# Six PSUM banks handed out first-free-first, in place of a rotating pool

## The chip, the cores and the metric

One Trainium2 chip, one of its cores. A core has a matrix engine (TensorE, PE in the profile, with the loading of its stationary operand as PEld), VectorE (DVE), ScalarE (ACT), GpSimd (POOL) and a queue that issues most of the loads (SyncE, SP). They run their own lists of instructions in order and wait for each other through semaphores. The results of PE go to PSUM, which has eight banks of 128 x 512 words; DVE and ACT read them from there. The metric is the device time of one launch in microseconds; the time before is the median of three runs, 481.18 us (481.16 to 481.39).

## What is computed

An RWKV-6 attention over 4 batches, 8 heads, 768 steps and a head size of 48, and behind it an MLP mixer over tokens and channels:

```python
for t in range(S):                       # S = 768
    cur = einsum('bhd,bhe->bhde', u[None] * k_t, v_t)
    y[:, :, t] = einsum('bhd,bhde->bhe', r_t, state + cur)
    state = w_t[:, :, :, None] * state + einsum('bhd,bhe->bhde', k_t, v_t)
x = y.transpose(0, 2, 1, 3).reshape(4, 768, 384)
h = maximum(x.transpose(0, 2, 1) @ w_tok1, 0.0) @ w_tok2     # 768 -> 256 -> 768
u = x + h.transpose(0, 2, 1)
out = u + maximum(u @ w_ch1, 0.0) @ w_ch2                    # 384 -> 1536 -> 384
```

## The kernel before

The attention is cut into twelve units (`unit(i)`), three to a batch, each of 256 steps in four chunks of 64. In a unit PE turns the keys (`turned_keys`, L344, two banks `k_ps`), adds keys times values to a running state (`outer`, L364, in a bank of its own, `kv_ps`), multiplies keys with queries (`grams`, L314, two banks `gram`), and forms the output from the states (`across`, L379) and from inside the chunk (`within`, L400), both in two banks `y_ps`. ACT copies the turned keys out (L349) and the output into the tile x (L406); DVE masks the grams (L487) and runs the scans over the decay (L434, L442) and the long multiplications (L439, L445).

The mixer of batch 0 is `mixing`. Those of batches 1 to 3 are `exact_mixing`, which splits float32 factors into rounded parts (names with `forms`, `high`, `low`, `joint`), so that each product is three cheaper passes. In its channel part each of twelve column blocks takes one bank `ends_ps` with nine matmuls: L739 and L741 (`end_passes`), L746 (`joint_passes`). ACT reads that bank with a rectification (L721, `high_of`), then DVE reads it once more (L728, `low_of`), and with that the bank is free. `down` (L757 to L759) sums six blocks into one bank `o_ps`, which DVE adds to x (L765). `back_half` (L693) fills banks `h_ps`, read by DVE (L696); `turn` (L708) fills banks `xT_ps`, read by ACT (L710) and DVE (L711). The third factor of L741 and L758 comes from memory through a ring of ten places (`load_third`, L625), a load being issued when PE has used up an earlier one.

The three units of batch 0 aside (batches are counted from 0), all of this runs interleaved: `first_mixing`, `exact_mixing`, `attention_pieces` and others give streams of pieces. A piece is a key, a function that issues instructions, and a list of operations (engine, time, what it needs, and behind that the names of the banks it takes; `("free", name)` where a bank is done with). The string `ORDER` says which stream gives the next piece; `interleaved` puts them in that order, and `strict` makes every engine keep it. Before the change `interleaved` uses only the function of each piece and drops the operations with their bank names.

The part ahead of L1061 (attention of batch 0 and the first mixer steps) uses two pools of two. At L1061 these are closed, and from there on one pool `ps_m` with six rotating buffers serves every allocation: `bank(name)` and some direct `ps_m.tile(...)` calls. The n-th allocation takes the bank of the (n-6)-th, and its first matmul waits until that one's last reader is done, whether other banks are free or not.

## Time and profile before

| | us |
|---|---|
| median of three runs | 481.18 |
| the profiled execution | 481.39 |
| its span, first to last instruction | 479.7 |
| PE busy | 460.9 |
| DVE busy | 337.8 |
| ACT busy | 255.6 |
| PE waiting for the first load of rk | 8.3 |
| PE waiting after 52 us (one wait) | 1.5 |

The span is shorter than the time by what lies around the first and last instruction. A row of the timeline gives start and duration in us, engine, line and operation, what is written from what, how many instructions are merged, and in brackets how long the engine was idle and what ended it. A row of the waits names who waited for whom, the total, how often, and the longest.

### The profile page before, as it was taken

To read this page: it belongs to the slowest core of one execution; us is meant where nothing else is said; L and a number is where in the kernel's file an instruction comes from. 1 tells how busy PE (TensorE), PEld (TensorE's weight loads), DVE (VectorE), ACT (ScalarE), POOL (GpSimd) and SP (SyncE) were. 2 spreads that over 40 slices of the span, in tenths; PEclk is the share of its full clock that TensorE was granted. 3 is DMA by queue.
4 is the path that set the end of the run, shared out by engine and by line. 5 is a ranking of instruction groups with operands and counts; after the bars stand their busy time and mean duration, and the time that the engine had idled before them with its cause. 6 is when DMAs were issued, how large, how long until landed. Compare 5 with 4: busy or idle time off the path is not lost.

```text
span 479.7 us, 12681 instructions
## 1 busy us (share of the span) xinstructions
PE 460.9 (96%) x5298; PEld 405.1 (84%) x5298; DVE 337.8 (70%) x478; ACT 255.6 (53%) x588; POOL 59.8 (12%) x58
## 2 busy tenths in 40 slices
PE   3799999999999999999998999999999999999995
PEld 2686588856797668999998979999999979999995
DVE  7999799898786687675596966677596556235341
ACT  6689776765777566351546555251747344134140
POOL 1000000000000001240404001250404003032130
PEclk9889999999999999999999999999999999999999
DMA  8855653855563747854577723394585412336331
GB/s 310 327 198 193 215 194 105 264 188 185 175 182 105 241 131 227 232 179 150 183 239 235 268 75 117 123 267 134 163 276 169 166 37 82 118 98 198 88 94 55
DMA packets 49407, 83.77 MB, mean 175 GB/s; under 512 B 4864, under 2 KB 40576, under 8 KB 49344
## 3 DMA queue, kind: packets, MB, share of 16 engines
q1 hardware_dynamic: 49056, 82.80, 54.2%
q8 instruction: 43, 0.70, 0.6%
q14 instruction: 20, 0.16, 0.1%
q10 hardware_dynamic: 288, 0.10, 0.1%
HBM read 71.87 MB, written 11.01 MB: 173 GB/s over the span
## 4 chain that ended last, share of the span: by engine, by line
PE 93%; ACT 3%; DMA 1%; issue 1%; SPq 0%; DVE 0%; DVEq 0%; ACTq 0%
PE h_ps L953 10%; PE o_ps L757 8%; PE ends_ps L746 8%; PE ends_ps L739 8%; PE ends_ps L741 8%; PE o_ps L759 8%; PE o_ps L758 8%; PE z_ps L942 7%; PE h_ps L662 5%; PE gram L314 4%; PE z_ps L938 3%; PE h_ps L693 3%; PE y_ps L400 2%; PE kv_ps L364 2%; PE y_ps L379 2%; PE k_ps L344 2%
## 5 line engine op out<-in xcount | busy, mean ns | idle before, releaser
L732 POOL TENSOR_TENSOR z_high<-z_high 128x384 fp32r<-128x384 f32 x48 | 58.6, 1227 | 403.9 <-DMA ring<-third 187.7
L721 ACT ACTIVATE z_high<-ends_ps 128x384 fp32r<-128x384 f32 x48 | 23.5, 490 | 62.9 <-PE ends_ps L746 62.6
L728 DVE SCALAR_TENSOR_TENSOR z_high<-ends_ps,z_high 128x384 fp32r<-128x384 f32 x48 | 26.4, 554 | 36.7 <-ACT z_high L721 36.7
L739 PE MATMUL ends_ps<-x_forms,forms 128*128 128x384 f32 x216 | 50.0, 339 | 1.5 <-DVE z_high L728 1.5
L500 ACT ACTIVATE before<-state,to_end 112x48 f32<-112x48 f32 x132 | 33.3, 325 | 31.8 <-DVE state L515 20.0
L746 PE MATMUL ends_ps<-z_more,forms 128*128 128x384 f32 x216 | 50.1, 340 | 0.0
L741 PE MATMUL ends_ps<-x_forms,ring 128*128 128x384 f32 x216 | 49.3, 337 | 0.0
L953 PE MATMUL h_ps<-wch,z 128*128 128x384 f32 x144 | 48.5, 489 | 0.0
L757 PE MATMUL o_ps<-forms,z_high 128*128 128x384 f32 x140 | 48.2, 344 | 0.0
L765 DVE SCALAR_TENSOR_TENSOR x<-o_ps,x 128x384 f32<-128x384 f32 x35 | 18.7, 551 | 40.5 <-PE o_ps L759 40.4
L759 PE MATMUL o_ps<-forms,z_high 128*128 128x384 f32 x140 | 47.2, 337 | 0.0
L758 PE MATMUL o_ps<-ring,z_high 128*128 128x384 f32 x140 | 47.1, 337 | 0.0
L953 PEld LDWEIGHTS h_ps<-wch,z 128*128 128x128 f32 x144 | 26.7, 190 | 17.0
L739 PEld LDWEIGHTS ends_ps<-x_forms,forms 128*128 128x128 f32 x216 | 38.4, 188 | 2.2 <-DVE z_high L728 1.8
L746 PEld LDWEIGHTS ends_ps<-z_more,forms 128*128 128x128 f32 x216 | 39.0, 188 | 0.0
L741 PEld LDWEIGHTS ends_ps<-x_forms,ring 128*128 128x128 f32 x216 | 38.5, 188 | 0.0
L942 PE MATMUL z_ps<-xT,wch 128*128 128x256 f32 x144 | 31.5, 380 | 0.0
L942 PEld LDWEIGHTS z_ps<-xT,wch 128*128 128x128 f32 x144 | 27.1, 190 | 3.7
L724 ACT ACTIVATE z_high<-z_high 128x384 fp32r<-128x384 f32 x48 | 25.3, 526 | 3.5
L757 PEld LDWEIGHTS o_ps<-forms,z_high 128*128 128x128 f32 x140 | 26.3, 188 | 0.3
L758 PEld LDWEIGHTS o_ps<-ring,z_high 128*128 128x128 f32 x140 | 26.3, 188 | 0.0
L759 PEld LDWEIGHTS o_ps<-forms,z_high 128*128 128x128 f32 x140 | 26.3, 188 | 0.0
(198 smaller groups left out, 927.0 us busy)
## 6 DMA issues: line engine op xcount, KB each, us to landing
ring<-third SPq DMA_DIRECT2D x144, 192.0 KB, 3.1
raw<-in_w_ch_dram SPq DMA_DIRECT2D x16, 512.0 KB, 4.7
rk<-in_rk_dram SPq DMA_DIRECT2D x36, 192.0 KB, 5.4
near<-in_near_dram SPq DMA_DIRECT2D x8, 768.0 KB, 5.3
w<-in_w_dram SPq DMA_DIRECT2D x10, 520.5 KB, 4.1
vt<-in_v_dram SPq DMA_DIRECT2D x12, 384.0 KB, 4.6
out_dram<-x SPq DMA_DIRECT2D x17, 192.0 KB, 2.6
third<-forms SPq DMA_DIRECT2D x12, 192.0 KB, 3.1
```

What stands on the lines that cost most here:

```text
L500: act.mul(t[:ROWS, a], state[bt, g][:ROWS, a], by_last(c, j)[:, a:a + 1])
L724: act.mul(z_form(jt, 2), z_form(jt, 0).bitcast(f32), 1.0 / BASE)
L728: dve.scalar_tensor_tensor(z_form(jt, 1), a, 0.0, z_form(jt, 0).bitcast(f32), op0=ALU.max, op1=ALU.subtract)
L732: pool.tensor_add(z_form(jt, 2), z_form(jt, 2).bitcast(f32), z_form(jt, 1).bitcast(f32))
L739: pe.matmul(a, up[m], xf(0)[:, m], start=m == 0, stop=False)
L741: pe.matmul(a, low[:, m], xf(1)[:, m], start=False, stop=False)
L746: pe.matmul(banks["a", jt], joint, xf(2)[:, m], start=False, stop=m == 2)
L757: pe.matmul(a, z[0], up, start=first, stop=False, skip_group_check=True)
L758: pe.matmul(a, z[1], held[bt, s, half, 1, jt], start=False, stop=False, skip_group_check=True)
L759: pe.matmul(a, z[2], joint, start=False, stop=last, skip_group_check=True)
L942: pe.matmul(ps, now["wch1"][:, m, ts(jt, 128)], xT[:, m, ts(s, SEG)], start=(m == 0), stop=(m == DM // 128 - 1))
L953: pe.matmul(ps, zs[s][:, jt, ts(n, 128)], now["wch2"][:, jt, :], start=(jt == 0), stop=(jt == NJ - 1))
```

## The change

After L1061 the pool has one buffer of each name, and six tiles, `bank0` to `bank5`, are made from it once and put in a list. `with_banks` wraps the function of each piece: it sets the names of the banks that the piece takes, `bank` pops the first of the list for each, and after the piece the banks named in its `free` operations go to the end of the list. The direct `ps_m.tile` calls of `mixing` go through `bank` as well. Waits now follow from the accesses to the six tiles, not from the release of a pool's buffer. Lines behind the new functions stand 22 or more further down (L739 is now L761, L746 is L768, L344 is L366).

```diff
+    free_banks, taken_as, due = [], {}, []
+
     def bank(name):
-        return ps_m.tile([128, 512], f32, name=name, tag="m")
+        if not free_banks:
+            return ps_m.tile([128, 512], f32, name=name, tag="m")
+        t = free_banks.pop(0)
+        if due:
+            taken_as.setdefault(due.pop(0), []).append(t)
+        else:
+            free_banks.append(t)
+        return t
+
+    def with_banks(key, f, ops):
+        names = [(key[0], n) for op in ops if op[0] != "free" for n in op[3:]]
+
+        def g():
+            due[:] = names
+            f()
+            assert not due
+            for op in ops:
+                if op[0] == "free":
+                    free_banks.append(taken_as[key[0], op[1]].pop(0))
+
+        return g
...
-                sums[i] = ps_m.tile([128, DM], f32, name="h1_ps", tag="m")
+                sums[i] = bank("h1_ps")[:, :DM]
...
-                ps = ps_m.tile([128, DM], f32, name="h_ps", tag="m")
+                ps = bank("h_ps")[:, :DM]
...
-                sums["z", s] = ps_m.tile([128, SEG], f32, name="z_ps", tag="m")
+                sums["z", s] = bank("z_ps")[:, :SEG]
...
-                sums[n] = ps_m.tile([128, DM], f32, name="h2_ps", tag="m")
+                sums[n] = bank("h2_ps")[:, :DM]
...
-        out = [next(left_of[int(n)])[1] for n in order]
+        out = [with_banks(*next(left_of[int(n)])) for n in order]
...
-    ps_g, ps_m = None, six_banks.enter_context(tc.tile_pool(name="ps_m", bufs=6, space=bass.MemoryType.PSUM))
+    ps_g, ps_m = None, six_banks.enter_context(tc.tile_pool(name="ps_m", bufs=1, space=bass.MemoryType.PSUM))
+    free_banks += [ps_m.tile([128, 512], f32, name=f"bank{n}") for n in range(6)]
```

No engine's instructions change their number or order (PE's 3471 matmuls among them). What changes is the bank that a group gets and the semaphores that its first instruction waits for. Two places on PE show it; the numbers behind the names are the tiles'.

The first is in the last of the four parts of six blocks that the channel mixer of batch 1 has: two key tiles are turned, and two blocks follow, the third and fourth of the part. Before:

```order
L344 MATMUL k_ps_3029<-ident_101,rk1_89 128x112 [waits DMAHW7_49,DMAHW0_49,DVE_49]
L344 MATMUL k_ps_3029<-ident_101,rk1_89 128x112 x3
L344 MATMUL k_ps_3030<-ident_101,rk1_89 128x112 x4
L739 MATMUL ends_ps_3052<-x_forms_1343,forms1_1298 128x384 [waits DVE_49]
L739 MATMUL ends_ps_3052<-x_forms_1343,forms1_1298 128x384 x2
L741 MATMUL ends_ps_3052<-x_forms_1343,ring2_2230 128x384 [waits DMAHW4_49]
L741 MATMUL ends_ps_3052<-x_forms_1343,ring2_2230 128x384 x2
L746 MATMUL ends_ps_3052<-z_more_2116,forms1_1298 128x384 x3
L739 MATMUL ends_ps_3067<-x_forms_1343,forms1_1298 128x384 [waits DVE_49]
```

And with the change:

```order
L366 MATMUL bank5_886<-ident_101,rk1_89 128x112 [waits DMAHW7_49,DMAHW0_49,DVE_49]
L366 MATMUL bank5_886<-ident_101,rk1_89 128x112 x3
L366 MATMUL bank4_885<-ident_101,rk1_89 128x112 [waits Activation_49]
L366 MATMUL bank4_885<-ident_101,rk1_89 128x112 x3
L761 MATMUL bank1_882<-x_forms_1307,forms1_1263 128x384 [waits DVE_49]
L761 MATMUL bank1_882<-x_forms_1307,forms1_1263 128x384 x2
L763 MATMUL bank1_882<-x_forms_1307,ring2_2148 128x384 [waits DMAHW4_49]
L763 MATMUL bank1_882<-x_forms_1307,ring2_2148 128x384 x2
L768 MATMUL bank1_882<-z_more_2042,forms1_1263 128x384 x3
L761 MATMUL bank5_886<-x_forms_1307,forms1_1263 128x384 [waits Activation_49]
```

The last row is the same matmul in both: before it waited for DVE, now it writes the bank that the first turned keys had a few rows above, and waits for ACT.

The second place is the last block of the same part in batch 2. Before:

```order
L746 MATMUL ends_ps_4415<-z_more_2116,forms1_1298 128x384 x3
L739 MATMUL ends_ps_4429<-x_forms_1343,forms1_1298 128x384 [waits DVE_49]
L739 MATMUL ends_ps_4429<-x_forms_1343,forms1_1298 128x384 x2
L741 MATMUL ends_ps_4429<-x_forms_1343,ring2_2230 128x384 [waits DMAHW4_49]
L741 MATMUL ends_ps_4429<-x_forms_1343,ring2_2230 128x384 x2
```

And with the change:

```order
L768 MATMUL bank1_882<-z_more_2042,forms1_1263 128x384 x3
L761 MATMUL bank4_885<-x_forms_1307,forms1_1263 128x384 [waits Activation_49]
L761 MATMUL bank4_885<-x_forms_1307,forms1_1263 128x384 x2
L763 MATMUL bank4_885<-x_forms_1307,ring2_2148 128x384 [waits DMAHW4_49]
L763 MATMUL bank4_885<-x_forms_1307,ring2_2148 128x384 x2
```

Here too a wait for DVE became one for ACT: the bank was a `y_ps` before, and ACT copies that out.

## The prediction

> **What bounds the kernel now.** I read the page first, for the engine that is never free and for the chain that ended last.

> ```profile
> span 479.7 us, 12681 instructions
> ...
> PE 460.9 (96%) x5298; PEld 405.1 (84%) x5298; DVE 337.8 (70%) x478; ACT 255.6 (53%) x588; POOL 59.8 (12%) x58
> ...
> PE 93%; ACT 3%; DMA 1%; issue 1%; SPq 0%; DVE 0%; DVEq 0%; ACTq 0%
> ```

> TensorE (PE) is busy for 460.9 of 479.7 us and holds 93% of the chain. The change touches neither the number nor the size of any matmul, so it can give or take only idle time of PE. Next came the busy time by stage. The stretch up to 52 us is the part before the six banks are set up, which the change does not reach.

> ```profile
> core 0: us, PE busy (x) PEld busy (x) DVE busy (x) ACT busy (x) POOL busy (x), PEclk, DMA share, GB/s
> 0.00:52.00 52.00, 39.85 (x1004) 30.13 (x1005) 45.37 (x51) 39.70 (x100) 1.27 (x10) 0.93 0.75 263
> 52.00:187.00 135.00, 134.89 (x1457) 100.11 (x1457) 114.36 (x147) 91.29 (x191) 0.00 (x0) 1.00 0.57 176
> 187.00:254.00 67.00, 67.00 (x670) 66.28 (x669) 46.77 (x72) 31.66 (x83) 17.34 (x13) 1.00 0.66 205
> 254.00:257.00 3.00, 1.50 (x9) 1.18 (x8) 2.69 (x3) 2.04 (x7) 1.28 (x2) 1.00 0.68 160
> 257.00:479.70 222.70, 217.64 (x2165) 207.41 (x2163) 128.55 (x208) 90.95 (x211) 39.94 (x35) 1.00 0.46 144
> ...
> 474.30 0.34 PE L781 MATMUL o_ps<-ring,z_more 128*128 128x384 f32 x1
> ```

> From 52 us on PE has 0.11 us free, then none, then 1.50 us between 254 and 257 us, then 5.06 us. The last is the tail: the last matmul ends at 474.30 + 0.34 = 474.64, which is 5.06 us before the end of the span. The granted clock is 1.00 all through. So the stage that the change reaches has a single hole. The view of waits, restricted to PE after 52 us, has one row, and it is that hole:

> ```profile
> PE ends_ps L739 <- DVE z_high L728: 1.5, 1, 1.5
> ```

> **What the hole is.** L739 is the first matmul of a new group; it reads x_forms and forms, long there, and starts a new bank. So the wait on VectorE's L728 (which writes z_high, but reads the old ends_ps) is a wait for a bank. The timeline around it:

> ```profile
> 250.49 0.70 PE L746 MATMUL ends_ps<-z_more,forms 128*128 128x384 f32 x3
> 251.22 0.49 ACT L721 ACTIVATE z_high<-ends_ps 128x384 fp32r<-128x384 f32 x1 [0.47 <-PE ends_ps L746]
> 251.55 2.32 DVE L442 TENSOR_TENSOR_SCAN w<-w,starts 112x1041 f32<-112x1041 f32 x1
> 252.84 0.86 ACT L349 COPY kT<-k_ps 128x384 f32<-128x384 f32 x2
> 253.90 1.86 DVE L445 TENSOR_TENSOR rk<-rk,w 112x1024 f32<-112x1024 f32 x1
> 254.09 0.69 PE L746 MATMUL ends_ps<-z_more,forms 128*128 128x384 f32 x3
> 255.68 1.01 DVE L728 SCALAR_TENSOR_TENSOR z_high<-ends_ps,z_high 128x384 fp32r<-128x384 f32 x2
> 256.28 0.79 PE L739 MATMUL ends_ps<-x_forms,forms 128*128 128x384 f32 x3 [1.50 <-DVE z_high L728]
> 257.45 0.69 PE L746 MATMUL ends_ps<-z_more,forms 128*128 128x384 f32 x3
> 257.97 0.68 PE L739 MATMUL ends_ps<-x_forms,forms 128*128 128x384 f32 x3
> 259.53 0.68 PE L739 MATMUL ends_ps<-x_forms,forms 128*128 128x384 f32 x3
> ```

> The group that ended at 250.49 + 0.70 = 251.19 was read by ScalarE (ACT) at 251.22, but its second reader, L728 on VectorE, stood behind a 2.32 us scan and a 1.86 us multiplication and began only at 255.68. In round-robin order that bank's turn came at the group of 256.28, five allocations later (two y, two k, one ends), so PE stood until L728 had read it.

> **The change part by part.** Nothing moves: every engine has the same instructions in the same order, on VectorE and the load queue with the same waits. What changes is which bank an allocation gets, and so which reader it waits for: 72 PE instructions, 45 on ACT, two on POOL.

> *Term 1, the hole.* In the new list that group takes the bank of k_ps, which the first of the two L349 copies frees at about 252.84 + 0.43 = 253.27. PE could go on as soon as it is done with the group before: L746 started at 254.09, and three matmuls at the group's own rhythm (257.97 to 259.53 is nine in 1.56, 0.173 each) put the next start at 254.61. 256.28 - 254.61 = 1.67; the profile's idle, counted from the modelled end, is 1.50. I take 1.6 us. The bounds from both sides are 0, if the next wait is as long, and 1.67 + 0.11 = 1.78, all idle time of that stage.

> *Where the stall goes.* Does PE, 1.6 us earlier, run into the next late read? The group of 257.97 becomes 256.37 and takes the bank of the second L349 copy, free at 252.84 + 0.86 = 253.70: 2.67 us to spare. The group of 259.53 becomes 257.93 and takes the very bank that was late. It is free after the first L728 of the pair, at 255.68 + 0.55 = 256.23, so 1.7 us to spare, and 1.24 even against the end of the pair at 256.69. Behind them stand sets of matmuls that themselves drive their readers: the readers come 1.6 us earlier too, since ACT is busy for 90.95 and VectorE for 128.55 of the last 222.70 us. Loads cannot be the next limit at once: PE has no wait on a DMA in that row of waits, and the ring loads are issued by what PE has finished, so they move with it.

> *Term 2, the other changed waits of PE.* For each one I took the end of the reader it now names, in the trace of before, and the start of the matmul. None would have held PE. The two closest are these:

> ```profile
> 364.73 0.47 ACT L406 COPY x<-y_ps 64x384 f32<-64x384 f32 x1
> 366.18 0.69 PE L739 MATMUL ends_ps<-x_forms,forms 128*128 128x384 f32 x3
> ...
> 284.45 0.56 DVE L671 SCALAR_TENSOR_TENSOR z_more<-h_ps,z_more 128x384 fp32r<-128x384 f32 x1 [0.79 <-ACT z_more L669]
> 285.74 1.38 PE L693 MATMUL h_ps<-z_more,z_high 128*128 128x384 f32 x7
> ```

> At 366.18 the group now takes a y bank, which ACT's last copy frees at 364.73 + 0.47 = 365.20: 0.98 us to spare. At 286.09 (the third L693 of its row, two steps of 0.173 after 285.74) the bank is free at 284.45 + 0.56 = 285.01: 1.08 us to spare. Cost 0; the cover is that 1 us, and if it were gone, each place would cost what ACT or VectorE is late beyond it.

> *Term 3, ACT and POOL.* ACT gets 13 more entries in its lists of waits (mostly L710, which now also names VectorE's last read of the same bank). The closest is this pair:

> ```profile
> 287.33 1.61 DVE L696 SCALAR_TENSOR_TENSOR x<-h_ps,x 128x384 f32<-128x384 f32 x3 [1.73 <-PE h_ps L693]
> 290.41 0.49 ACT L710 ACTIVATE x_forms<-xT_ps 128x384 fp32r<-128x384 f32 x1 [0.36 <-PE xT_ps L708]
> ```

> L696 ends at 287.33 + 1.61 = 288.94, 1.47 us before L710 starts, and PE itself had to see the same read before it wrote the bank. Cost 0, covered by ACT's free 131.75 us of the last 222.70; if that cover were gone, each of the 13 could at most double the 0.36 us that such an L710 already stands there for, 4.7 us of ACT in all, still a small part of what it has free.

> *Sum.* The profiled execution took 481.39 us, with 1.69 us around its span; 481.39 - 1.6 = 479.79. The median of the three runs shown is 481.18, 0.21 below the profiled one; 481.18 - 1.6 = **479.6 us**. A measurement of this kernel can tell about 0.2% from no change, 0.96 us, so the line between faster and same lies at 480.22.

> **The rivals.** *A: the gain is mostly taken back at the next late read.* For it: VectorE is at its fullest there, 2.69 of 3.00 us, and PE has used up the lead that let it run ahead. Against it: the margins of 2.67, 1.7 and 1.24 us. If VectorE comes to that pair later by one more scan (2.32 us), the group of 259.53 waits 2.32 - 1.24 = 1.08 us, and of the 1.6 only 0.52 is left: 481.18 - 0.52 = 480.7 us. That counts as no change.

> *B: slower, because a bank comes back sooner than in strict rotation.* The mechanism: first-free-first goes by the order of the pieces, not by the time at which a reader is done, and can hand a y or k bank to an ends group soon after its copy is issued. Place: the attention units, where a y bank is passed to an ends group (366.18, margin 0.98; in round-robin the same group waited for an L728 that had ended at 363.12, 3.07 us before). It decides once ACT's copies come later than now by more than 0.98 us. Price: one hole such as today's, 1.50 us, at every second of the six units of the last two batches: 3 x 1.5 - 1.6 = 2.9, so 484.1 us; for one such hole the balance is 481.18 - 1.6 + 1.5 = 481.1. Against it: between 187 and 474 us ACT is busy for under half of the time, and its order has not changed.

> [...]

> *C: the change does nothing here*, because the wait at 256.28 has a second condition as late as L728. For it: a wait is put down to the last of several. Against it: in the order of before, the only wait on that L739 is for VectorE. 481.2 us.

> **How the numbers follow.** My forecast, 479.6 us, gets 0.79 and its own range is 479.2 to 480.2 (1.78 us and the 0.2 us by which the runs differ on one side, the line of 480.22 on the other). Rival A has 0.11, C has 0.03, B has 0.07, of which 0.02 for the single hole that leaves no change. Faster 0.79, same 0.11 + 0.03 + 0.02 = 0.16, slower 0.05. The range takes the forecast and most of A: 479.2 to 480.7 us.

> **What would show it.** Right: the view of PE's waits after 52 us is empty; the group of 256.28 starts near 254.6; every later matmul stands 1.6 us earlier; the busy time of PE is still 460.9; the tail is still 5.06. Wrong step by step: a new row of PE waiting on L728 or L406 (A or B), the row still there (C), or matmuls of the same line that take longer than now. The forecast as a whole falls if PE's busy time changes by more than half a microsecond, for then banks matter to the matmuls themselves, of which no row of before tells anything.

## The result and the profile after

The changed kernel took 479.34 us (median of 22 runs) beside 481.34 us for the one before in the same 22 rounds; the ratio, with disturbed runs left out, is 0.9952 with a 95% interval of 0.9936 to 0.9967. Two more sets of 12 runs of the same kernel gave 0.9973 (0.9957 to 0.9988) and 0.9968 (0.9953 to 0.9983). Weighted by their runs the three make 0.9962, or 1.8 us of 481.2. The forecast was 1.6 us faster, 479.6; by the first set alone 481.18 x 0.9952 = 478.9, which is under the low end of 479.2.

The page of the changed kernel, its chain by engine among it:

```profile
span 479.1 us, 12687 instructions
...
PE 459.6 (96%) x5298; PEld 404.6 (84%) x5298; DVE 338.0 (71%) x478; ACT 255.8 (53%) x588; POOL 59.8 (12%) x58
...
PE 92%; DMA 3%; ACT 2%; issue 1%; DVE 1%; SPq 1%; DVEq 0%; ACTq 0%
```

By stage (columns as in the table of the prediction; L761 is L739 of before, L768 is L746, L336 is L314):

```profile
0.00:52.00 52.00, 38.34 (x1002) 29.31 (x1003) 44.64 (x50) 38.99 (x100) 1.27 (x10) 0.97 0.77 264
52.00:187.00 135.00, 135.00 (x1458) 100.07 (x1457) 114.83 (x148) 91.85 (x190) 0.00 (x0) 1.00 0.56 176
187.00:254.00 67.00, 65.88 (x660) 65.02 (x659) 45.53 (x71) 30.30 (x77) 15.74 (x13) 1.00 0.66 200
254.00:257.00 3.00, 3.00 (x22) 3.00 (x22) 2.97 (x2) 3.00 (x12) 2.28 (x1) 1.00 0.98 257
257.00:479.10 222.10, 217.41 (x2164) 207.18 (x2162) 130.01 (x211) 91.62 (x213) 40.51 (x35) 1.00 0.47 145
```

The 1.50 us that PE lacked between 254 and 257 us are filled. But the stretch ahead of it, full before, now lacks 1.12. The view of PE's waits after 52 us has again one row, another one:

```profile
PE bank L336 <- issue: 1.1, 1, 1.1
```

"issue" is time in which the engine waited for nothing that the profile shows. The timeline has it in the middle of a row of grams, where no bank begins and no semaphore is waited for:

```profile
239.21 0.54 PE L336 MATMUL bank<-rk 48*64 48x64 f32 x21
240.87 0.85 PE L336 MATMUL bank<-rk 48*64 48x64 f32 x41 [1.12 <-issue]
```

And this is the place of the old hole, 1.6 us later in the span because of that pause and of the first 52 us:

```profile
253.15 2.32 DVE L464 TENSOR_TENSOR_SCAN w<-w,starts 112x1041 f32<-112x1041 f32 x1
254.44 0.86 ACT L371 COPY kT<-bank 128x384 f32<-128x384 f32 x2
255.50 1.86 DVE L467 TENSOR_TENSOR rk<-rk,w 112x1024 f32<-112x1024 f32 x1
255.70 0.69 PE L768 MATMUL bank<-z_more,forms 128*128 128x384 f32 x3
256.22 0.69 PE L761 MATMUL bank<-x_forms,forms 128*128 128x384 f32 x3
257.29 0.55 DVE L750 SCALAR_TENSOR_TENSOR z_high<-bank,z_high 128x384 fp32r<-128x384 f32 x1
```

VectorE comes to its late read (L750, L728 of before) behind the same scan and the same multiplication, only at 257.29; PE's next group began at 256.22, 0.52 us after the start of the last three matmuls ahead of it, and did not wait.

Laid over each other matmul by matmul (PE's order is the same in both), the two traces differ in few places. Start in the change less start before, in us, and the step at each place:

```
at before   line   difference   step
  45.71     L896      +0.69     +0.80   the first 52 us, pause "issue"
 151.62     L314      +0.26     -0.29   grams, pause "issue"
 239.27     L314      +1.60     +1.33   grams, pause "issue"
 256.28     L739      -0.06     -1.67   the hole
 256.56     L739      -0.17     -0.11   the matmuls behind the hole, 0.79 to 0.69
 span end             -0.59
```

So the hole was worth 1.67 + 0.11, unrounded 1.77 us. In this one execution a pause at a matmul that begins no bank, 1.33 us longer here than in the profile of before, took most of it back. The medians show that this execution, 480.81 us, was slower than most of its kernel.

### The profile page after: what moved, and what is told of

It is laid out like the page before. It is cut to its first block, busy times and chain, and to the rows that moved or that the text cites. A ratio compares the mean times of both kernels' runs of the same rounds, so it can differ in the third digit from the quotient of the medians.

```text
span 479.1 us, 12687 instructions
## 1 busy us (share of the span) xinstructions
PE 459.6 (96%) x5298; PEld 404.6 (84%) x5298; DVE 338.0 (71%) x478; ACT 255.8 (53%) x588; POOL 59.8 (12%) x58
## 4 chain that ended last, share of the span: by engine, by line
PE 92%; DMA 3%; ACT 2%; issue 1%; DVE 1%; SPq 1%; DVEq 0%; ACTq 0%
PE bank L975 10%; PE bank L768 8%; PE bank L761 8%; PE bank L779 8%; PE bank L763 8%; PE bank L781 8%; PE bank L780 8%; PE bank L964 7%; PE bank L684 5%; PE bank L960 3%; PE bank L715 3%; PE bank L336 2%; PE bank L401 2%; PE bank L422 2%; PE kv_ps L386 2%; DMA w<-in_w_dram 2%
## 5 line engine op out<-in xcount | busy, mean ns | idle before, releaser
L750 DVE SCALAR_TENSOR_TENSOR z_high<-bank,z_high 128x384 fp32r<-128x384 f32 x48 | 26.4, 553 | 35.0 <-ACT z_high L743 35.0
L768 PE MATMUL bank<-z_more,forms 128*128 128x384 f32 x216 | 50.1, 340 | 0.0
L761 PE MATMUL bank<-x_forms,forms 128*128 128x384 f32 x216 | 49.9, 339 | 0.0
L763 PE MATMUL bank<-x_forms,ring 128*128 128x384 f32 x216 | 49.4, 337 | 0.0
L975 PE MATMUL bank<-wch,z 128*128 128x384 f32 x144 | 48.5, 489 | 0.0
L779 PE MATMUL bank<-forms,z_high 128*128 128x384 f32 x140 | 48.2, 344 | 0.0
L781 PE MATMUL bank<-forms,z_high 128*128 128x384 f32 x140 | 47.2, 337 | 0.0
L780 PE MATMUL bank<-ring,z_high 128*128 128x384 f32 x140 | 47.1, 337 | 0.0
L975 PEld LDWEIGHTS bank<-wch,z 128*128 128x128 f32 x144 | 26.7, 190 | 17.0
L768 PEld LDWEIGHTS bank<-z_more,forms 128*128 128x128 f32 x216 | 39.0, 188 | 0.0
L761 PEld LDWEIGHTS bank<-x_forms,forms 128*128 128x128 f32 x216 | 38.5, 188 | 0.4
L763 PEld LDWEIGHTS bank<-x_forms,ring 128*128 128x128 f32 x216 | 38.6, 188 | 0.0
L746 ACT ACTIVATE z_high<-z_high 128x384 fp32r<-128x384 f32 x48 | 25.3, 526 | 3.8 <-ACT z_high L743 0.4
L779 PEld LDWEIGHTS bank<-forms,z_high 128*128 128x128 f32 x140 | 26.3, 188 | 0.3
L781 PEld LDWEIGHTS bank<-forms,z_high 128*128 128x128 f32 x140 | 26.3, 188 | 0.0
```

Of the source, the lines that this page charges most:

```text
L746: act.mul(z_form(jt, 2), z_form(jt, 0).bitcast(f32), 1.0 / BASE)
L750: dve.scalar_tensor_tensor(z_form(jt, 1), a, 0.0, z_form(jt, 0).bitcast(f32), op0=ALU.max, op1=ALU.subtract)
L761: pe.matmul(a, up[m], xf(0)[:, m], start=m == 0, stop=False)
L763: pe.matmul(a, low[:, m], xf(1)[:, m], start=False, stop=False)
L768: pe.matmul(banks["a", jt], joint, xf(2)[:, m], start=False, stop=m == 2)
L779: pe.matmul(a, z[0], up, start=first, stop=False, skip_group_check=True)
```

## What the words ahead of the prediction had wrong

They say that the pool of before hands the bank of the (n-6)-th allocation to the n-th. It does not. These are the first eleven allocations after L1061 as the built program of before has them:

```
tile  h  h  xT h  xT h  xT h  xT z  z
bank  2  7  6  5  4  3  2  6  4  7  5
```

In rotation the eighth would be bank 7. It is bank 6, of the first xT, which ACT has read by 56.00 us in the trace, while bank 7 is read by VectorE until 56.74; 4 (56.38) comes next, then 7, then 5 (57.20). And around the hole the two y banks, still in use, are passed over. Here the pool followed the order in which the banks in fact came free, which neither of the two rules of this document does. At the hole it did not: it gave out the bank that VectorE read at 255.68 ahead of the two that ACT had read by 253.70. The explanation of the hole from the trace does not depend on the rule; the word "round-robin" in the prediction is wrong. Over the 261 allocations after L1061 the bank is that of the sixth allocation before in 51% of the cases; with the change it is so in 48%.

## The experiments

**Both lists of banks, with and without the one late bank.** The first kernel has the six fixed tiles, but each allocation takes the bank that it had before, from a written list. In it and in the second, one bank passes on before its last read in the order of the pieces: at the first unit of batch 3 the copy of the turned keys (L349) reads what the next group has put there, so batch 3 is computed from other keys, with the same work. The copy starts at 286.40 us where before has 284.31; PE does not wait for it.

```diff
-        t = free_banks.pop(0)
...
-        return t
+        return free_banks[int(next(in_order, 0))]
...
-        out = [with_banks(*next(left_of[int(n)])) for n in order]
+        out = [next(left_of[int(n)])[1] for n in order]
```

> The six tiles are made once, but every allocation gets the bank that it had before the change, from a written list. Theory (the whole gain is the one hole at 256 us): the hole of 1.5 us on PE's L761 is back, ratio to before 1.000. Rival (the way the waits are derived, from accesses to six fixed tiles and not from the release of a pool's buffers, gives a part of its own): faster than before by about 0.5 us, ratio 0.999, with the hole still there.

Ratio 1.0008 (0.9990 to 1.0026). The hole is back, in PE's waits after 52 us:

```profile
PE bank L749 <- DVE z_high L738: 1.5, 1, 1.5
```

The second kernel exchanges two numbers of that list from the block at 256 us on, so that the order of the banks changes only there.

> The same list with one exchange: the block at 256 us takes the bank of the turned keys, the next block the bank that is read late; from there on the two numbers are exchanged. Theory: all of the gain, no wait of PE after 52 us, ratio 0.9965 (1.67 us of 481.2) or a little less. Rival (the gain is spread over many changed waits): 0.999 to 1.000, and the hole moves to the next block.

Ratio 0.9970 (0.9951 to 0.9988), and no wait of PE after 52 us at all. One bank exchanged for another in one place out of 261 brings what the whole change brings. The third starts from the list of the change and gives the late bank back to that block:

> The list of banks that the change gives, with one exchange: the block at 256 us takes the late bank again. Theory: the hole of 1.5 us is back and the time is that of before, ratio 1.000. Rival (72 changed waits each give a little): the gain stays but for the hole, ratio about 0.998.

Ratio 1.0005 (0.9990 to 1.0021), with the same wait of 1.5 us. So the other changed waits bring nothing that these intervals can tell, and neither do the fixed tiles.

**The changed kernel again**, twice, for the spread and the pause.

> The changed kernel once more, for a second profile and a second set of times. Theory: no wait of PE on a bank; the 1.1 us for which PE stood in the middle of the grams at 239.8 us in the first profile, with nothing to wait for, is not there again, and the ratio is 0.9963, above the 0.9952 of the first set. Rival (the first set was right as it stands): 0.995.

> The changed kernel a third time, for a third profile and a third set of times. Theory (hole of 1.77 us gone, pause amid the grams 0.4 to 1.3 us in this kernel and near 0 in the one before): ratio 0.996 to 0.9985 by the terms, no wait of PE on a bank after 52 us. Rival (the first set as it stands): 0.995.

The ratios stand at the top. In all three profiles the hole is gone by the same step of 1.67 us, and the pause is there in each, of three lengths: a step of 1.33, 0.46 and 1.03 us at the same matmul. The second profile:

```profile
PE bank L336 <- issue: 0.5, 2, 0.3
```

**The kernel before against itself.**

> The kernel before, unchanged, against itself: how far two sets of times of one kernel lie apart, and a second profile. Theory (the 1.1 us for which PE stood amid the grams at 239.8 us in the first profile of the change, with nothing to wait for, differs from one execution to the next and has nothing to do with the banks): ratio 1.000 within its interval, the hole of 1.5 us at 256 us, and a pause of 0 to 1.3 us amid the grams near 239 us or near 151 us. Rival (the pause comes with the six fixed tiles): no such pause here.

Ratio 0.9998 (0.9984 to 1.0012). Its second profile has the hole and a small pause near 152 us, and next to none near 239, as the first had:

```profile
PE ends_ps L739 <- DVE z_high L728: 1.5, 1, 1.5
PE gram L314 <- issue: 0.3, 1, 0.3
```

Two profiles of one kernel, with spans of 479.7 and 481.2 us, differ by 1.5 us, nearly what the change brings. The greater part of it lies in the first 52 us, where the granted clock was 0.93 in the one and 0.90 in the other, and 0.97 in the first profile of the change.

**Taking the cause away instead.** The kernel before, its pool as it was; in the order string VectorE's late read comes ahead of the scan, and with it on PE the block ahead of the hole comes before the turned keys (L344):

```diff
-    "000500050000000000455547455555555450045555000505600640000000576666666560000000000000000066050006066600066666000666666006"
+    "000500050000000000455547455555555450045555000505600640000000576500006666666000000000000066050006066600066666000666666006"
```

VectorE's list there is now:

```
L728 SCALAR_TENSOR_TENSOR z_high<-ends_ps
L728 SCALAR_TENSOR_TENSOR z_high<-ends_ps
L442 scan
L445 TENSOR_TENSOR rk<-rk,w
L728 SCALAR_TENSOR_TENSOR z_high<-ends_ps
```

> The kernel before with its own pool of six buffers; in the order of the pieces only, VectorE's late read of the bank (L728 of the eighth block) and the block ahead of it come before the scan and the multiplication of the attention unit. Theory (the hole is VectorE's place in line, not the number or the order of the banks): no wait of PE after 52 us, 1.6 us faster, ratio 0.9965. Rival (the pool's way of handing out banks is what costs): the hole is there again or moves to another block, ratio 1.000.

Ratio 0.9975 (0.9957 to 0.9992), no wait of PE after 52 us. The pool hands out other banks at 67 of the 261 places, but by the built program the block that stood in the hole, here at 255.40 us, still takes the bank of the late read and still waits for VectorE. The second read begins at 252.63, ahead of the scan at 253.10:

```profile
252.63 0.56 DVE L728 SCALAR_TENSOR_TENSOR z_high<-ends_ps,z_high 128x384 fp32r<-128x384 f32 x1 [0.19 <-ACT z_high L721]
253.10 2.70 DVE L442 TENSOR_TENSOR_SCAN w<-w,starts 112x1041 f32<-112x1041 f32 x1
```

> The changed kernel with the same move in the order of the pieces. Theory: there is one hole to take away, so the two do not add up; ratio 0.9965, as for each alone. Rival (the change gives something else besides the hole): 0.993.

Ratio 0.9963 (0.9946 to 0.9980): the two do not add up to 0.993, which lies outside. There was one thing to win, and either way wins it.

**What another order of the same six tiles costs.** The rival by which banks make the kernel slower, in its own kernel:

```diff
-        t = free_banks.pop(0)
+        made_at[None] = made_at.get(None, 0) + 1
...
+        oldest = min(range(len(free_banks)), key=lambda n: made_at.get(id(free_banks[n]), 0))
+        t = free_banks.pop(oldest)
+        made_at[id(t)] = made_at[None]
```

> The changed kernel, but of the free banks the one that was handed out longest ago is taken, not the one freed longest ago. This prices the slower rival of the prediction. Theory (which bank comes next matters where a reader is late): PE waits for banks at some eight places after 52 us, for about 8 us in all by the margins of the trace of before, so 489 us, ratio 1.017. Rival (any order of six banks does): the time of before or better.

Ratio 1.0210 (1.0167 to 1.0252), 491.97 us, from four runs. PE's waits after 52 us, all but the last row shown:

```profile
PE bank L784 <- DVE x L792: 3.5, 1, 3.5
PE bank L784 <- DVE at L514: 1.7, 2, 0.9
PE bank L766 <- DVE z_high L755: 1.1, 1, 1.1
PE bank L980 <- ACT x L433: 1.1, 1, 1.1
PE bank L341 <- issue: 1.0, 2, 0.8
PE bank L729 <- ACT kT L376: 0.9, 1, 0.9
```

Six waits for banks make 8.3 us of these, with the one of 0.5 us left out 8.8. So this order of banks cost ten microseconds. This kernel, which comes nearest to a rotation (in 71% of its allocations the bank is that of the sixth before), is the slowest of the bank orders tried, and the change, which goes by the order of freeing, has no wait on a bank after 52 us. A strict rotation was not run.

**What the pause is.** Counting PE's list in the trace (a weight load, a matmul and a wait of its own are a record each), over its three profiles the long pauses outside of waits lie at records 1985, 4033 and 5825 in the change: each is 193 more than a multiple of 256. The page lists a DMA queue by the kind "instruction":

```profile
q8 instruction: 43, 0.70, 0.6%
```

```diff
+    def ahead():
+        for _ in range(16):
+            pe.matmul(kv[0:1, 1, 400:401], least, least, start=True, stop=True, skip_group_check=True)
...
-    strict(lambda: load_part(0, 1), masks,
+    strict(ahead, lambda: load_part(0, 1), masks,
```

> The changed kernel with 16 one-by-one matmuls ahead of everything, in the 8 us in which PE waits for its first load; they write a word of a bank that nothing reads, and move all of PE's later instructions 64 records further in its list. Theory (the pause amid the grams near 239 us sits at every 256th record of PE's list, wherever that falls): it moves back by 64 records, out of the second half of the grams into their first half or the kv matmuls ahead of them, and the hole stays away. Rival (the pause belongs to these grams, their data or their banks): it stays at the same matmul.

Ratio 1.0213 (1.0185 to 1.0240), 491.51 us, from six runs, as in the next.

```profile
PE bank L422 <- issue: 4.5, 3, 1.9
PE bank L975 <- issue: 2.3, 1, 2.3
```

> The same with 32 such matmuls, 128 records. Theory: the pause falls into the kv matmuls ahead of the grams, and the one at 151 us moves in the same way. If the pauses are shorter there, the ratio falls below that of the change (0.996) by up to 0.002. Rival: same matmul, same time as the change.

Ratio 1.0463 (1.0433 to 1.0494), 504.35 us.

```profile
PE bank L422 <- issue: 7.7, 4, 3.8
PE bank L336 <- issue: 3.5, 1, 3.5
PE bank L779 <- DVE at L509: 3.1, 1, 3.1
```

> The changed kernel with 64 one-by-one matmuls ahead, 256 records, within the 8 us in which PE waits for its first load. Theory (what cost 10 and 23 us with 64 and 128 records is where every 256th record of PE's list falls): a whole step of 256 puts them on the same matmuls as in the change, so the time is that of the change again, ratio 0.996 to 0.998. Rival (the matmuls put ahead cost by themselves, by their number): 45 us more, ratio 1.09.

Ratio 0.9970 (0.9950 to 0.9990), 480.00 us. With a shift of 256 records the time is that of the change (0.9962 over its three sets); with 64 and 128 it is 10 and 23 us longer than before. The pauses did not go where my expectation for 64 put them (the first half of the grams or the kv matmuls): the block of 256 records that ended amid the grams now ends in kv without a pause, and the next one ends in the y matmuls (L422), after only 1.85 us, with a step of 2.1 us; two more blocks ending there have 1.5 and 1.6. In all of these profiles each pause of over 0.8 us that no semaphore explains is again at 193 past a multiple of 256 (1473 to 8641, 961 to 9409, 2241 to 6081). The hope that another place would be cheaper was wrong.

## Why the prediction was right or wrong

**What bounds the kernel: right.** One hole of PE in the stage that the change reaches, and nothing else for the banks to win there. One exchanged bank gives 0.9970, the whole change 0.9962 over three sets.

**Term 1, the hole: right in kind, small by a tenth.** I took 1.6, between 1.50 and 1.67. Start to start it measured 1.67 in every profile that has PE's order as it was and no wait there, and the first matmuls behind the hole, which took 0.79 us where others take 0.68, lost their 0.11 as well: 1.77. Its row was quoted, and I did not read it as part of the price.

**Where the stall goes: right.** The next late reads were passed with room to spare; no wait on a bank is left after 52 us.

**Terms 2 and 3: right.** Cost 0 for the other waits: the list of the change with the one late bank put back is at 1.0005. ACT's added waits show in no wait of PE.

**What failed is the range, at the words "the 0.2 us by which the runs differ on one side".** Three runs of before lay within 0.23 us. Of 22, the lowest is 479.83, and all but one (486.22) are at or below 482.67. The first 52 us alone moved the rest by -1.4 to +1.2 us from profile to profile, and the pauses at records 193 past a multiple of 256 by up to 1.3 us at one place. A range of half a microsecond below the forecast was a claim about a spread that three runs cannot carry. The later two sets, 0.9973 and 0.9968, are 1.3 and 1.5 us, near the 1.6; the first, 0.9952, is 2.3 with an interval from 1.6 to 3.1. What the first set has beyond the 1.77 us of the hole no trace shows; that it fell under 479.2 and the other two did not is, as far as is known, the draw of the runs. All three together, 0.9962, give 479.4, inside the range.

**The check by PE's busy time was a bad one.** I wrote that the forecast falls if it changes by more than half a microsecond. It went from 460.9 to 459.6, but the kernel before has 460.9 in one profile and 462.6 in the next. In the stage of the banks (52 to 470 us) the sums are 416.39 before and 416.88 after; what differs beyond the hole is the first 52 us, at a varying clock. The tail came out at 479.1 - (474.07 + 0.34) = 4.69 us against 5.06; over the profiles of these bank orders it is 4.6 to 5.3.

**The rivals.** A, that the gain is taken back at the next late read, did not happen; something that no term had, the pause amid the grams, took part of it back in the profiles: 0.46 to 1.33 us near 239 us, where the three profiles with the pool of before (one of them early_read's) show under 0.2. The other kernels with six tiles have it too, later256 at 1.0, but for one_swap, which shows none. Whether that is so on average stays open: the kernels with six tiles and the hole are at 1.0008 and 1.0005, some 0.3 us slower than before, with intervals of about 0.8 us to either side. B exists, at 2.1%, for another rule of picking a bank, not for this one. C is out.

**The 23 us of 128 records** were not foreseen. Laid over the first profile of the change as above, they are 12.1 us in pauses at records 193 past a multiple of 256 behind 52 us, 6.0 in three stretches with a granted clock of 0.5 (from 132.3, 279.0 and 391.7 us, 3.4 to 6.8 us long), 3.1 in the wait on VectorE and 2.7 in the first 52 us, less the change's own pause of 1.3. The 10 us of 64 records are 7.5 in the pauses, 3.3 at half the clock and 0.8 in the first 52 us, less the same 1.3. In both 0.2 us are left over.

## What to carry to other kernels

Where PE is full but for one wait on a bank, look at which reader is late and where it stands in its engine's line: here a second reader behind a scan of 2.32 us and a multiplication of 1.86 held a bank for 4.5 us after the first reader (251.71 to 256.23 us), while two others came free at 253.27 and 253.70. Giving that one group another bank (0.9970), or moving that one read with the block ahead of it (0.9975), brought what the whole rewriting of the allocator did (0.9962). And before a change of 0.3% is believed or doubted, run the unchanged kernel against itself: here 16 or 32 tiny matmuls ahead of everything cost 2 and 5%, and two profiles of one kernel differ by nearly as much as the change brings.

## What the runs showed of the hardware that was not expected

The queue of kind "instruction" had 43 packets of 16,384 bytes before and with the change, and 44 packets on its page with 128 records more. At records 193 past a multiple of 256 PE stood, in some places, with nothing in the views of waits but "issue": for 1.12 us at 240.87 us in the change's first profile, up to 3.8 us in one place with 128 records more. There, too, it went on after the end of a packet: the packet took from 130.83 to 131.75 us, and PE went on at 133.11. In the change the packet ahead of 240.87 ran from 237.90 to 239.38; in the profile of before it ran from 235.96 to 237.19, and PE did not stand at 239.23. Why it came earlier there stays open. Not every short block of 256 records pauses: two of 1.71 us in the change, ending at 125.39 and 345.99 us, did not, nor did the same two in its other profiles. That PE waits for such a packet is how I read these times; no run shows it apart from them.

The granted clock after 52 us was 1.00 in the profiles of before and the change, the hole of 1.84 us between two starts and the pause of 1.34 among them, until the last matmul. It was not with 128 records more:

```profile
100.00:200.00 100.00, 95.06 (x1087) 67.18 (x1086) 72.88 (x96) 61.41 (x139) 0.00 (x0) 0.97 0.52 160
200.00:300.00 100.00, 95.42 (x1078) 90.55 (x1077) 69.16 (x100) 47.84 (x119) 20.96 (x16) 0.98 0.65 197
300.00:501.00 201.00, 192.48 (x1755) 186.15 (x1753) 107.71 (x180) 75.05 (x176) 36.53 (x32) 0.99 0.43 130
```

Each of the three holds one of the stretches at 0.5 named above, from 132.3, 279.0 and 391.7 us, the first of them inside PE's idle time of 3.81 us that ended at 133.11. After 52 us the fourteen profiles have six places where 2.1 to 4.0 us lie between the starts of two matmuls: L422 (idle 1.9 us) and L975 (2.3) with 64 records more, L422 (3.8), L336 (3.5) and L779 (3.1) with 128, and L784 (3.5) in the kernel that takes the bank handed out longest ago. Beside each of them the profile has a stretch at 0.5 of 3.4 us or more. That the long idle time brings the low clock no run was made to show.
